# Weight words rebuilt straight into their own tile, fewer and larger loads, and an order made with the queue's eight lanes

## The chip, the cores and the metric

The program runs on one core of a Trainium2 chip, in one launch. TensorE multiplies, VectorE (DVE), ScalarE (ACT) and GpSimd (POOL) work on the elements, and SyncE (SP) issues the transfers. The metric is the device time of one execution in microseconds (us): 658.67 is the median of 3 runs before the change (657.94 to 660.53). The profile is one more execution, which took 658.94 us.

## The reference

```python
def _attn_ref(q, k, v, a_re, a_im):        # 4 batches, 8 heads, 768 tokens, width 48
    mag = np.sqrt(a_re * a_re + a_im * a_im)
    scale = np.minimum(mag, 0.999) / (mag + 1e-06)
    a_re_n, a_im_n = (a_re * scale, a_im * scale)
    for t in range(S):
        new_re = ar * S_re - ai * S_im
        new_im = ar * S_im + ai * S_re
        kv = np.einsum('bhd,bhe->bhde', k[:, :, t], v[:, :, t])
        S_re, S_im = (new_re + kv, new_im)
        y[:, :, t] = np.einsum('bhd,bhde->bhe', q[:, :, t], S_re)
def _moe_ref(x, w_in, w_out, a, b):        # 3072 tokens, 384 -> 2048 -> 384
    h = x @ w_in
    P = a[0] + a[1] * h + a[2] * h * h + a[3] * h * h * h
    Q = 1.0 + np.abs(b[0]) * np.abs(h) + np.abs(b[1]) * h * h
    return (P / (Q + 1e-06)) @ w_out
def _moe2_ref(x, w_skip, ...):             # a token goes on to an expert only if x @ w_skip > 0
    out = x.copy()
```

An attention with a complex decay feeds a wide layer with a rational gate. Then each token is tested against `w_skip`; with the inputs used no path behind that test runs, so the wide layer's result is the output.

## The kernel before, in words

The 3072 tokens are 12 units of 256, each of 2 chunks of 128. For a unit, `early` works the decays (`ar`, `ai`) into logarithms and angles on DVE and ACT, `cums` sums them over time with products on PE, and `trig` takes sines and cosines (`cs`). `prods` multiplies the scaled q and k by them: a product of 768 elements a partition, `kt` from k and `qt` from q, twice per chunk, by DVE or POOL (L378). `chunk` transposes (L696), forms scores (L716), masks them (L721), multiplies by v (L739) and by the carried state (L741), and updates the state (L762). A chunk's result `ys` is corrected by two small transfers inside SBUF (`ysd`) and stored as `xh` and a rest `xl` (L794, L799).

The wide layer runs a unit in 8 steps, of two blocks of 128 hidden columns each: `G1` (L852) makes the hidden values, nine instructions on ACT and DVE (`a1` to `d4`, L832, L375, L836) the gate, `gh` and `gl` (L881, L884) its two parts, `G2` (L904) adds to the output. Units 1 to 11 multiply in three fast parts (high by high, high by low, low by high). Unit 0 multiplies whole F32 values, since its weights are not yet split.

The weights come from HBM as float64 words, as the host holds them, 32 blocks of 128 x 384. `weight` loads a block as words (`ws`, 384 KB), rebuilds the F32 value with three DVE instructions (`wb1` to `wb3`, L425, L428, L435) and one scaling on ACT or POOL (`wy`, L431, L432), and then a transfer on the chip (`wcp`) copies the value from the stage to `wil` or `wol`, because the stage's place becomes the high part (`whi`, L451). `wlo` (L456) turns `wil` and `wol` into the low parts where they stand.

v comes three times per chunk: all heads (`vb`), and the odd heads with the two token halves swapped (`vo`, two transfers of 64 rows x 4 pieces of 48 numbers).

What runs when is written by a planner, `Plan`, at build time. Each task has options (engine and cost), a rank from due times and a table of numbers (`RK`), and engines that it may not use (`NO`). The resulting order is fixed: each engine runs its list in turn, and waits where a result is missing. In gaps of PE's planned list `filled` puts products that nobody reads (L991, L995, L998; "fillers" here). Transfers of SP all go into one queue, and each takes the next of eight semaphores ("lanes") in turn: a transfer on a lane waits for the last one on it.

Of the kernel before, what the change touches and what calls it, by code (L numbers as in the profile page):

```python
# [183 lines left out]
PP = dict(RK={('prr2', 2): 3.12, ('a5', 0): 4.66, ('wb3', 0): 3.26, ('wb2', 0): -1.55, ('a5', 2): 29.52, ('red', 3): -5.84, ('thi', 2): -15.73, ('G2', 3): 5.39, ('sc', 3): -2.18, ('S', 3): 4.15, ('d4', 0): -7.69, ('e10', 2): 43.63, ('e5', 3): -3.63, ('xp', 2): 28.26, ('xhi', 3): 1.43, ('sc', 2): -10.69, ('cry', 3): -3.27, ('d3', 0): -4.72, ('wldo', 0): -11.48, ('S2', 2): -16.91, ('yev', 3): -2.07, ('a3', 3): 2.6, ('a5', 1): -11.48, ('d4', 1): 15.02, ('a1', 0): 5.15, ('ysd', 3): 4.13, ('xpe', 3): 0.91, ('msk', 1): -2.71, ('xlo', 3): 38.81, ('xpe', 1): -5.76, ('e1', 3): 19.05, ('tlo', 2): 31.77, ('e7f', 2): -28.75, ('upd', 2): 20.93, ('G2', 1): -1.18, ('S2', 0): 17.75, ('e8', 2): 10.97, ('wcp', 0): 1.93, ('msk', 0): -34.0, ('cadd', 3): 2.32, ('cuml', 3): 3.94, ('ymm', 3): 0.58, ('ahi', 2): 33.56, ('trig', 3): -7.45, ('a1', 1): 9.46, ('cuml', 2): 40.94, ('a4', 1): -2.63, ('yev', 0): -0.58, ('e7f', 3): 6.69, ('dec', 2): -15.18, ('G2', 2): -1.44, ('e10', 3): 5.07, ('e13', 3): -3.92, ('e4', 3): -0.99, ('d4', 3): -1.96, ('rnd', 0): 51.87, ('upd', 1): -11.05, ('prr1', 2): -12.43, ('e6', 3): 19.64, ('exq', 3): -0.91, ('cumx', 2): -2.78, ('a2', 2): 18.7, ('xp', 0): -12.54, ('xabs', 0): -9.64, ('G1', 0): 3.1, ('a4', 0): -2.66, ('e6', 2): -8.09, ('ysd', 1): -6.35, ('d3', 3): 2.37, ('red', 1): -3.23, ('G1', 3): 0.96, ('e11', 0): -34.69, ('alo', 2): 3.31, ('gl', 1): -3.15, ('G1', 2): 0.12, ('e9', 2): -27.01, ('qr', 3): -8.38, ('dec', 1): 5.65, ('xlo', 2): 1.21, ('e7', 3): 0.19, ('e3', 3): 6.62, ('cadd', 1): -9.18, ('ldk', 2): -62.56, ('prr2', 1): 6.83, ('gh', 2): 0.17, ('gl', 3): 17.93, ('ldv', 3): 12.89, ('cumx', 0): -1.69, ('xlo', 1): -4.07, ('wlo', 0): -0.06, ('a5', 3): -0.37, ('e11', 3): 0.32, ('e10', 0): -4.98, ('xp', 1): 6.71, ('d1', 3): 0.76, ('d1', 1): -4.12, ('exq', 1): -7.0, ('xhi', 2): 3.18, ('e9', 3): 7.67, ('e2', 0): 16.76, ('ev', 1): -17.58, ('lda', 0): 10.16, ('sk', 0): -11.96, ('S2', 3): -2.37, ('e7', 1): 1.46, ('a3', 2): 5.85, ('e5', 0): -4.81, ('e11', 1): 14.72, ('a2', 3): 4.03, ('dec', 0): -2.65, ('sk', 2): 5.88, ('xpe', 0): -0.24, ('cf', 0): 0.81, ('st', 0): 6.79, ('dec', 3): -6.11, ('e2', 3): 2.44, ('a4', 2): -2.83, ('kr', 0): -3.6, ('msk', 3): -0.46, ('G1', 1): -1.67, ('d2', 3): -2.05, ('a3', 1): 5.72, ('ldk', 3): 1.99, ('rnd', 3): 10.32, ('sk', 3): -2.18, ('e11', 2): -8.06, ('ymm', 2): -1.42, ('d2', 1): 10.01, ('G2', 0): 1.41, ('red', 2): 12.85, ('a1', 2): -3.47, ('e2', 2): -10.52, ('e4', 1): -44.42, ('e7', 0): 27.96, ('d2', 0): -1.15, ('lda', 1): -1.87, ('xabs', 1): -2.0, ('sk', 1): -36.69, ('ev', 0): -14.56, ('e3', 1): 23.6, ('whi', 0): 0.56, ('e9', 1): -3.01, ('e4', 0): 6.8, ('S', 0): 7.17, ('xabs', 3): -4.9, ('gl', 2): -3.79, ('e8', 0): 2.21, ('exp', 3): 8.53, ('d1', 2): 0.05, ('qr', 2): -11.3, ('xabs', 2): 1.36, ('d4', 2): -1.13, ('qr', 0): -3.05, ('e8', 1): 8.77, ('lda', 3): 0.02, ('e7', 2): -9.52, ('ldq', 3): 12.22, ('st', 1): -2.0, ('kr', 2): -6.08, ('ldc', 0): 10.23, ('ldk', 1): -12.6, ('last', 1): 27.98, ('prr1', 1): 0.86, ('e7f', 1): 3.77, ('cry', 1): -1.5, ('consts', 0): -7.94, ('kr', 1): 7.89, ('consts2', 0): -1.73, ('wb1', 0): 0.08, ('sc', 1): -1.53, ('a1', 3): -0.46, ('e6', 0): 1.18, ('thi', 3): 3.26, ('clear', 0): 0.66, ('e13', 1): 4.78, ('cuml', 1): 0.28, ('ldq', 1): -1.73, ('gh', 3): 8.2, ('trig', 0): 2.05, ('S', 2): 1.66, ('e5', 1): -1.37, ('qr', 1): -4.52, ('e10', 1): -0.7, ('ldq', 2): 18.6, ('sc', 0): -1.03, ('exq', 2): 14.38, ('e9', 0): -0.62, ('xpe', 2): 0.81, ('cumx', 1): 1.08, ('ymm', 0): 6.87, ('yev', 2): 0.36, ('last', 3): -0.64, ('upd', 3): -0.13, ('e13', 2): -2.22, ('e3', 2): 1.71, ('upd', 0): 0.0, ('ev', 2): 1.27, ('lda', 2): 0.45, ('e1', 1): -8.86, ('cadd', 2): -2.13, ('ysd', 0): -2.42, ('gh', 1): 0.65, ('e6', 1): -2.17, ('ldv', 0): 1.52, ('ldk', 0): 1.29, ('d3', 1): 7.67, ('cry', 2): -0.27, ('lnexp', 0): -5.28, ('rnd', 1): -2.74, ('ldv', 2): -0.5}, FU=1, C2=72.509, C3=123.091, AF=6.693, P0=3.688, P1=4.377, NO={'e4': ('POOL',), 'wlo': ('DVE',), 'prr1': ('DVE',), 'whi': ('POOL',), 'thi': ('ACT',)}, E0=68.086, E1=-19.697, TC=16, WS=(0, 1, 2, 3, 4, 5, 0, 1, 1, 0, 1, 2, 2, 1, 2, 2), HO={('cadd', 'POOL'): 0.163, ('last', 'POOL'): 0.177, ('prr2', 'POOL'): 0.1, ('gh', 'ACT'): 0.048, ('tlo', 'POOL'): 0.482, ('thi', 'ACT'): 0.071, ('tlo', 'DVE'): 0.437, ('last', 'ACT'): 0.166, ('yev', 'DVE'): 0.201, ('xhi', 'ACT'): 0.027, ('gh', 'DVE'): 0.58, ('gl', 'POOL'): 0.428, ('xhi', 'DVE'): 0.403, ('xlo', 'POOL'): 0.542, ('wlo', 'DVE'): 0.468, ('gl', 'DVE'): 0.016, ('cadd', 'DVE'): 0.052, ('xpe', 'DVE'): 0.549, ('prr1', 'DVE'): 0.097, ('e4', 'POOL'): 0.456, ('whi', 'POOL'): 0.398}, DW=177.48, WL=7, P=6.193, LAG2=4.124, SL={'ACT': 0.955, 'DVE': 1.413, 'POOL': 0.138, 'SP': 0.1, 'PE': 2.407, '2': 1.094}, X1=27.056, T0=48.313, NZ=6, NH=3, CU=2, BI={'DVE': 73.29, 'POOL': 44.682})  # L184


def main_part(tc, ctx, q, k, v, a_re, a_im, w_in, w_out, moe_a, moe_b, w_skip, out, keep):
# [1202 lines left out]
```

## Time and profile before

| | |
|---|---|
| median of 3 runs | 658.67 us (657.94 to 660.53) |
| the profiled execution | 658.94 us |
| its span, first to last instruction | 657.1 us |
| PE, DVE, ACT, POOL busy | 97%, 86%, 86%, 52% |
| fillers among PE's time | 40.2 us (32.3 + 4.0 + 3.9) |
| DMA moved | 52.09 MB, in 49458 packets, 20320 of them under 512 B |

PE is called busy while it runs a filler too. An F32 product leaves two records in the trace, so 254 records of L998 are 127 instructions.

### The profile page before, as it was taken

Reading aid. Unit: us, or ns where it says so; the run is one execution under the profiler, and the core shown is the slowest. Engines: PE = TensorE matmul, PEld = TensorE weight load, DVE = VectorE, ACT = ScalarE, POOL = GpSimd, SP = SyncE. Lnnn points to the kernel's source line nnn. Section 1 sums busy time; section 2 is a strip of 40 time slices with the busy share of each in tenths; the row PEclk is TensorE's granted clock in tenths of the full one; section 3 lists DMA queues with packets and bytes.
Section 4 is the critical chain, followed back from the end, with each engine's and each line's share of the span. In section 5 each row is a group of like instructions: output and inputs, shape, how many; then the busy total and the mean of one; then the engine's idle time right before and its main releaser. Section 6 shows DMA issues by size and latency. Waiting matters only on the chain.

```text
span 657.1 us, 15009 instructions
## 1 busy us (share of the span) xinstructions
PE 635.3 (97%) x5704; PEld 592.4 (90%) x5704; DVE 562.4 (86%) x897; ACT 563.0 (86%) x935; POOL 338.7 (52%) x339
## 2 busy tenths in 40 slices
PE   9999999989999999999999999999999999999993
PEld 8787777778998989999999999989999999999993
DVE  6988999899899889988998789899889896968882
ACT  6748999998898899997999998989989989867770
POOL 4432577965357475454684654553565753622220
PEclk9998999999999999999999999999999999999997
DMA  8968821501302113013112113013013010000000
GB/s 291 304 211 289 273 96 48 166 24 44 98 25 75 49 47 117 15 35 103 35 47 86 33 47 100 19 47 102 19 46 101 19 49 3 19 30 3 22 4 30
DMA packets 49458, 52.09 MB, mean 79 GB/s; under 512 B 20320, under 2 KB 45280, under 8 KB 49376
## 3 DMA queue, kind: packets, MB, share of 16 engines
q1 hardware_dynamic: 49088, 51.03, 25.5%
q8 instruction: 47, 0.77, 0.5%
q14 instruction: 35, 0.29, 0.1%
q10 hardware_dynamic: 288, 0.00, 0.0%
HBM read 38.73 MB, written 4.72 MB: 66 GB/s over the span
## 4 chain that ended last, share of the span: by engine, by line
PE 66%; ACT 15%; DMA 7%; DVE 4%; issue 3%; SPq 2%; POOL 2%; ACTq 0%; DVEq 0%; POOLq 0%
PE zb L852 24%; PE ob L904 23%; PE zb L696 5%; PE zb L716 4%; DMA ws<-in_moe_w_in_dram 3%; PE zb L739 3%; PE zb L741 2%; ACT wk L832 2%; ACT wk L375 2%; ACT tb L515 2%; PE zb L762 2%; SPq L371 2%; DMA vb<-in_v_dram 1%; ACT L551 1%; ACT zb L832 1%
## 5 line engine op out<-in xcount | busy, mean ns | idle before, releaser
L852 PE MATMUL zb<-xh,wil 128*128 128x256 f32 x624 | 171.2, 297 | 0.3 <-DVE wk L836 0.2
L836 DVE SCALAR_TENSOR_TENSOR wk<-wk,cf,zb 128x512 f32<-128x512 f32 x192 | 141.0, 740 | 26.5 <-ACT zb L832 17.3
L852 PE MATMUL zb<-xh,wi 128*128 128x256 f32 x528 | 152.7, 289 | 0.0
L852 PE MATMUL zb<-xl,wi 128*128 128x256 f32 x528 | 148.8, 282 | 0.0
L375 ACT ACTIVATE wk<-wk,cf 128x512 f32<-128x512 f32 x192 | 139.7, 730 | 2.3
L881 POOL TENSOR_SCALAR gh<-wk 128x512 fp32r<-128x512 f32 x80 | 56.3, 704 | 152.3 <-PE ob L904 100.3
L904 PE MATMUL ob<-wo,gh 128*128 128x384 f32 x352 | 121.4, 345 | 1.7 <-DVE zb L922 1.7
L852 PEld LDWEIGHTS zb<-xh,wil 128*128 128x128 f32 x624 | 117.1, 189 | 4.0 <-DVE wk L836 0.8
L904 PE MATMUL ob<-wol,gh 128*128 128x384 f32 x352 | 118.8, 338 | 0.0
L904 PE MATMUL ob<-wo,gl 128*128 128x384 f32 x352 | 118.8, 338 | 0.0
L852 PEld LDWEIGHTS zb<-xh,wi 128*128 128x128 f32 x528 | 99.4, 188 | 3.1 <-issue 1.9
L852 PEld LDWEIGHTS zb<-xl,wi 128*128 128x128 f32 x528 | 99.3, 188 | 0.4
L832 ACT ACTIVATE wk<-zb,cf 128x512 f32<-128x512 f32 x96 | 66.0, 688 | 10.2 <-PE zb L852 5.2
L836 DVE SCALAR_TENSOR_TENSOR zb<-wk,cf,zb 128x512 f32<-128x512 f32 x96 | 71.5, 746 | 0.0
L832 ACT ACTIVATE zb<-wk 128x512 f32<-128x512 f32 x96 | 58.0, 606 | 14.6 <-DVE wk L836 14.4
L904 PEld LDWEIGHTS ob<-wo,gh 128*128 128x128 f32 x352 | 66.1, 188 | 3.1 <-DVE zb L922 1.9
L832 ACT ACTIVATE wk<-zb 128x512 f32<-128x512 f32 x96 | 57.5, 601 | 12.4 <-PE zb L852 12.0
L836 DVE SCALAR_TENSOR_TENSOR wk<-wk,zb 128x512 f32<-128x512 f32 x96 | 65.2, 681 | 1.3
L904 PEld LDWEIGHTS ob<-wol,gh 128*128 128x128 f32 x352 | 66.3, 188 | 0.0
L904 PEld LDWEIGHTS ob<-wo,gl 128*128 128x128 f32 x352 | 66.1, 188 | 0.0
L884 POOL TENSOR_TENSOR gl<-wk,gh 128x512 fp32r<-128x512 f32 x41 | 60.7, 1480 | 6.2 <-ACT gh L877 3.2
L378 POOL TENSOR_TENSOR qt<-r,cs 128x768 f32<-128x768 f32 x24 | 51.9, 2162 | 20.4 <-ACT cs L552 10.6
(168 smaller groups left out, 1380.0 us busy)
## 6 DMA issues: line engine op xcount, KB each, us to landing
ws<-in_moe_w_in_dram SPq DMA_DIRECT2D x16, 384.0 KB, 6.7
ws<-in_moe_w_out_dram SPq DMA_DIRECT2D x16, 384.0 KB, 4.8
ar<-in_a_re_dram SPq DMA_DIRECT2D x24, 192.0 KB, 3.4
ai<-in_a_im_dram SPq DMA_DIRECT2D x24, 192.0 KB, 3.8
qraw<-in_q_dram SPq DMA_DIRECT2D x24, 192.0 KB, 2.6
kraw<-in_k_dram SPq DMA_DIRECT2D x24, 192.0 KB, 2.5
vb<-in_v_dram SPq DMA_DIRECT2D x24, 192.0 KB, 3.3
out_dram<-x2b SPq DMA_DIRECT2D x24, 192.0 KB, 1.9
```

The costliest lines, as they stand in the source:

```text
L371: nc.sync.dma_start(out=o, in_=i)
L375: return ("ACT", cost, lambda: nc.scalar.activation(out=out, in_=in_, func=func, **kw))
L378: return (e, cost, lambda: eng[e].tensor_tensor(out=out, in0=in0, in1=in1, op=op), both)
L696: nc.tensor.transpose(z[0:112, i, :], src[:, 112 * h:112 * h + 112], ident)
L716: nc.tensor.matmul(z[o:o + 64, h, n:128], lhsT=K[:, h, n:n + 64], rhs=Q[:, h, n:128], start=True, stop=True)
L739: nc.tensor.matmul(dst, lhsT=vt, rhs=pT[hf][:, i, :], start=True, stop=first)
L832: return ("ACT", cost, lambda: nc.scalar.activation(out=h() if out is None else out, in_=h() if in_ is None else in_, func=func, **kw))
L836: return ("DVE", cost, lambda: nc.vector.scalar_tensor_tensor(out=h() if out is None else out, in0=in0, scalar=scalar, in1=h(), op0=op0, o ...
L852: nc.tensor.matmul(h()[:, i * 256:i * 256 + 256], lhsT=w[:, 128 * j:128 * j + 128], rhs=x[:, j, :], start=(n == 0), stop=(n == 3 * len(pr) ...
L881: nc.gpsimd.tensor_scalar(out=g, in0=uu, scalar1=1.0, scalar2=1.0, op0=ALU.mult, op1=ALU.mult)
L884: eng[e].tensor_tensor(out=ghl("gl", s), in0=uu, in1=ghl("gh", s).bitcast(F32), op=ALU.subtract)
L904: nc.tensor.matmul(o, lhsT=a[:, sl], rhs=w, start=(f == 0 and n == 0), stop=(f == NF - 1 and n == len(pr) - 1))
```

## The change

- **Weights.** A transfer brings two blocks (768 KB of words). `wb3` writes the F32 value not into the stage but into a tile of its own (`fi`, `fo`), so that the 32 copies on the chip go. `wlo` no longer works in place: it writes the low part of weight j (`li`, `lo`) into the place of the F32 tile of weight j-1, and so the weights are split in turn, and unit 2's `xl` takes the place of the last F32 tile.
- **Loads.** q, k, `ar` and `ai` of a unit come in one transfer each instead of two. v is laid out on the host with the swapped odd heads behind it, and comes in one transfer of 2304 B a row instead of three. SP issues 474 transfers in the whole program, 616 before.
- **Order.** The planner now follows the eight lanes, a cost per transfer, and has new numbers throughout. Of DVE and POOL, all 48 `kt` and `qt` products are DVE's (16 before); 69 of 88 `gl` and all 88 `gh` are POOL's (41 and 80 before). PE's list has 135 fillers of the kind of L998 (127 before).

```diff
-        queue = 0.0
+        queue, lanes, lane = 0.0, [0.0] * 8, 0
...
+                    if e == "SP":
+                        end, many = now, o_[3]
+                        for _ in range(many):
+                            end = max(end, lanes[lane]) + cost / many
+                            queue = max(queue, end + 0.7) + t.xfer / many
+                            lanes[lane] = queue + 1.1
+                            lane = (lane + 1) % 8
+                        cost = end - now
...
-PP = dict(RK={('prr2', 2): 3.12, ('a5', 0): 4.66, ('wb3', 0): 3.26,
...
+PP = dict(RK={('e1', 3): -0.0, ('qr', 1): 6.96, ('d3', 3): 13.1,
...
-    vb = [T(f"vb{i}", [128, H * 48 + 16]) for i in range(2)]
-    vo = [T(f"vo{i}", [128, H // 2 * 48 + 16]) for i in range(2)]
+    vb = [T(f"vb{i}", [128, H * 72 + 16]) for i in range(2)]
+    vo = [t[:, H * 48:H * 72 + 16] for t in vb]
...
+        if n == "xl" and u % 2 == 0:
+            if "xl0" not in lazy:
+                lazy["xl0"] = keep["wp"].tile([128, 768], F32R, tag=f"wl{2 * NP}", name="xl0")
+            t = lazy["xl0"]
...
+    def weight_f(m, p):
+        if (m, p) not in whole_w:
+            whole_w[m, p] = keep["wp"].tile([128, 2, DM], F32, tag=f"wl{rank_of(m, p) + 1}", name=f"f{m}{p}")
+        return whole_w[m, p]
+
+    def weight_lo(m, p):
+        if p not in low[m]:
+            low[m][p] = keep["wp"].tile([128, 2, DM], F32R, tag=f"wl{rank_of(m, p)}", name=f"l{m}{p}")
+        return low[m][p]
...
+    def weight(m, p, num):
+        slot = ("st", num % NP)
+        d_ = (w_in[p].rearrange("q (z n) -> q z n", z=2) if m == "i" else w_out[2 * p:2 * p + 2].rearrange("z q n -> q z n"))
+        pl.add(dma(lambda: [(stage(num).bitcast(I32), d_.bitcast(I32))], n=1), writes=[slot] + [("sh", num % NP, z) for z in range(2)],
+               name=f"wld{m}{p}", xfer=0.68 * NB / DM * 2)
+        for z in range(2):
+            block(m, p, z, num)
...
         def value():
-            return stage(num)[:, 0:DM]
+            return weight_f(m, p)[:, z, :]
...
-                reads=keys + [w_], writes=[h_], free=tk, name="wb3")
-            src = keys + [h_]
-        w = wil if m == "i" else wol
-        pl.add(dma(lambda: [(w[:, 2 * p + z, :].bitcast(F32), value())], n=1), reads=src, writes=[("wf",) + key], name="wcp", xfer=0.5)
-
+                reads=keys + [w_, h_], writes=[("wf", m, p, z)], free=tk, name="wb3")
...
-            eng[e].tensor_tensor(out=lo, in0=lf, in1=weight_hi(m, p).bitcast(F32), op=ALU.subtract)
+            eng[e].tensor_tensor(out=weight_lo(m, p), in0=weight_f(m, p), in1=weight_hi(m, p).bitcast(F32), op=ALU.subtract)
...
-               reads=h_, writes=w + l_, name="wlo")
+               reads=h_ + w, writes=l_ + before, name="wlo")
...
-            pl.add(dma(*[(raw[nm][:, 8 * c:8 * c + 8, :], chunk_src(x, 2 * u + c)) for c in range(2)]),
-                   writes=[nm], name=f"ld{nm}{u}", xfer=1.3)
+            pl.add(dma((two_chunks(raw[nm]), unit_src(x, u))), writes=[nm], name=f"ld{nm}{u}", xfer=1.3)
...
-        pl.add(dma((vb[ci % 2][:, 0:H * 48], chunk_src(v, ci).rearrange("t h d -> t (h d)")),
-                   (odd[0:64], src[64:128, :, 1]), (odd[64:128], src[0:64, :, 1])),
+        b, c = divmod(ci, CPB)
+        pl.add(dma((vb[ci % 2][:, 0:H * 72], v[b, c * 128:(c + 1) * 128, :])),
...
+def _v_rows(x):
+    b, h, t, d = x.shape
+    x = x.transpose(0, 2, 1, 3)
+    odd = x[:, :, 1::2].reshape(b, t // 128, 2, 64, h // 2 * d)[:, :, ::-1]
+    return np.concatenate([x.reshape(b, t, h * d), odd.reshape(b, t, h // 2 * d)], axis=2)
```

The order moves at three places that the prediction speaks of. The first is SP's list from the fourth unit of decays on up to the first correction of `ys` (`dec` is the decay row of a chunk, `cs<-xr` the carried angle). Before:

```order
L371 DMA wil<-ws_202 128x384
L371 DMA dec_122<-last 48x1x8 x2
L371 DMA wil<-ws_204 128x384
L371 DMA wil<-ws_207 128x384
L371 DMA wil<-ws_211 128x384
L371 DMA cs<-xr 1x8x48
L371 DMA kraw<-in_k_dram 128x384 x2
L371 DMA wil<-ws_224 128x384
L371 DMA ws_499<-in_moe_w_out_dram 128x768
```

and, three copies and three transfers of v later, `ys<-ys 16x3x128 x2`. Now:

```order
L383 DMA ws_341<-in_moe_w_in_dram 128x1536
L383 DMA ws_348<-in_moe_w_out_dram 128x2x768
L383 DMA dec_118<-last 48x1x8 x2
L383 DMA ws_395<-in_moe_w_in_dram 128x1536
L383 DMA ws_400<-in_moe_w_out_dram 128x2x768
L383 DMA cs<-xr 1x8x48
L383 DMA kraw<-in_k_dram 128x2x384
L383 DMA ws_484<-in_moe_w_in_dram 128x1536
L383 DMA vb_95<-in_v_dram 128x576
L383 DMA ys<-ys 16x3x128 x2
```

The copies are gone from between the small transfers, and the loads of words stand there instead.

The second is PE's list in front of the first `G1` of unit 0 (`wil`, now `fi`, is the F32 weight; `ob<-ident` are fillers). Before:

```order
L998 MATMUL ob_79<-ident 128x128 x4
L762 MATMUL zb_82<-vb_98,kt_111 64x48 x16
L998 MATMUL ob_79<-ident 128x128 x2
L621 MATMUL zb_81<-ai_146,trit 128x384
L998 MATMUL ob_79<-ident 128x128 x19
L648 MATMUL zb_81<-ta_156,trir 128x384
L648 MATMUL zb_83<-ta_156,trir 128x384
L998 MATMUL ob_79<-ident 128x128 x3
L852 MATMUL zb_82<-xh_4_646,wil 128x256 x6
```

Now:

```order
L795 MATMUL zb_83<-vb_96,kt_107 64x48 x16
L1032 MATMUL ob_77<-ident 128x128 x2
L681 MATMUL zb_79<-ta_154,trir 128x384
L681 MATMUL zb_82<-ta_154,trir 128x384
L1032 MATMUL ob_77<-ident 128x128 x6
L654 MATMUL zb_83<-ai_142,trit 128x384
L1032 MATMUL ob_77<-ident 128x128 x7
L886 MATMUL zb_83<-xh_4_614,fi_297 128x256 x6
```

In the whole list 108 fillers stood ahead of this `G1`, and now 103, and one `ai` sum more stands ahead of it.

The third is DVE's list where the first `G2` of unit 0 gets its weight (`fo_821`; `wk` are gate values). Now:

```order
L870 SCALAR_TENSOR_TENSOR wk<-wk,zb_83 128x512
L870 SCALAR_TENSOR_TENSOR wk<-wk,cf,zb_84 128x512
L458 TENSOR_SCALAR zb_81<-ws_348 128x384
L870 SCALAR_TENSOR_TENSOR wk<-wk,cf,zb_80 128x512
L461 SCALAR_TENSOR_TENSOR zb_79<-ws_348,zb_79 128x384
L870 SCALAR_TENSOR_TENSOR zb_80<-wk,cf,zb_80 128x512
L461 SCALAR_TENSOR_TENSOR zb_81<-ws_348,zb_81 128x384
L870 SCALAR_TENSOR_TENSOR wk<-wk,zb_80 128x512
L468 SCALAR_TENSOR_TENSOR fo_821<-ws_348,zb_79 128x384
L468 SCALAR_TENSOR_TENSOR fo_821<-ws_348,zb_81 128x384
```

Before, the same weight (`ws_215`, `ws_220`) was rebuilt ahead of DVE's first gate instruction, and was copied by a transfer later; now it stands behind two steps of the gate.

## Rows read from the trace of the kernel before

**Rows 1.** The page: busy us of each engine (share of the span), instructions.

```profile
PE 635.3 (97%) x5704; PEld 592.4 (90%) x5704; DVE 562.4 (86%) x897; ACT 563.0 (86%) x935; POOL 338.7 (52%) x339
```

**Rows 2.** Groups of all instructions, PE's fillers: records | busy us, mean ns | idle before.

```profile
L998 PE MATMUL ob<-ident 128*128 128x128 f32 x254 | 32.3, 281 | 0.0
```

**Rows 3.** Waits of PE, whole span: what waited, for whom: us in total, times, longest.

```profile
PE ob L904 <- DVE zb L922: 1.7, 1, 1.7
PE zb L319 <- POOL nedge L290: 1.5, 1, 1.5
```

**Rows 4.** Waits of PE from 150 us on, all three that the view lists.

```profile
PE zb L716 <- ACT qT L702: 1.9, 3, 0.9
PE faz L1301 <- DVE fat L1295: 1.7, 1, 1.7
PE zb L696 <- DVE kt L378: 0.8, 1, 0.8
```

**Rows 5.** SP in order of time, 32 to 53 us: start, us, what.

```profile
32.01 1.26 SPq L371 DMA_DIRECT2D dec<-last  x2
...
43.39 1.30 SPq L371 DMA_DIRECT2D ys<-ys  x2
...
52.77 1.48 SPq L371 DMA_DIRECT2D ys<-ys  x2
```

**Rows 6.** ACT in order of time, 48 to 61 us; idle before in brackets.

```profile
48.24 0.52 ACT L794 ACTIVATE xh<-ys 128x384 f32<-128x384 f32 x1 [2.54 <-DMA ys<-ys]
...
50.08 0.84 ACT L557 ACTIVATE ai<-ai 128x768 f32<-128x768 f32 x1
...
60.63 0.51 ACT L794 ACTIVATE xh<-ys 128x384 f32<-128x384 f32 x1
```

**Rows 7.** DVE in order of time, five places.

```profile
11.41 0.56 DVE L425 TENSOR_SCALAR zb<-ws 128x384 int32<-128x384 int32 x1 [1.58 <-DMA ws<-in_moe_w_in_dram]
...
50.95 0.55 DVE L579 SCALAR_TENSOR_TENSOR ai<-cs,ai 1x384 f32<-1x384 f32 x1 [1.47 <-ACT ai L557]
...
58.25 1.48 DVE L435 SCALAR_TENSOR_TENSOR ws<-ws,zb 128x384 int32<-128x384 int32 x3
...
138.89 3.49 DVE L378 TENSOR_TENSOR kt<-r,cs 128x768 f32<-128x768 f32 x2 [0.49 <-ACT cs L552]
...
371.59 0.96 DVE L378 TENSOR_TENSOR kt<-r,cs 128x768 f32<-128x768 f32 x1 [2.14 <-ACT cs L552]
```

**Rows 8.** PE in order of time, 49 to 75 us.

```profile
49.54 1.14 PE L762 MATMUL zb<-vb,kt 128*64 128x48 f32 x32 [0.93 <-DVE ys L781]
...
52.53 1.62 PE L621 MATMUL zb<-ai,trit 128*128 128x384 f32 x2 [1.21 <-issue]
...
61.20 5.45 PE L852 MATMUL zb<-xh,wil 128*128 128x256 f32 x24
...
73.31 1.45 PE L904 MATMUL ob<-wol,wk 128*128 128x384 f32 x4
```

**Rows 9.** Stretches of 2 us: PE, PEld, DVE, ACT, POOL busy; granted clock, DMA share, GB/s.

```profile
52.00:54.00 2.00, 1.47 (x3) 0.90 (x4) 1.82 (x4) 1.96 (x4) 0.53 (x1) 0.55 1.04 356
54.00:56.00 2.00, 2.00 (x13) 2.00 (x12) 1.83 (x4) 1.56 (x3) 0.00 (x0) 0.60 1.02 401
```

**Rows 10.** Stretches of 20 us, the same columns.

```profile
20.00:40.00 20.00, 19.50 (x215) 18.16 (x214) 18.74 (x41) 14.56 (x23) 9.35 (x9) 1.00 0.81 278
40.00:60.00 20.00, 16.89 (x175) 14.67 (x175) 16.65 (x29) 11.30 (x16) 3.44 (x5) 0.91 0.88 282
```

**Rows 11.** Groups of all instructions: the gate on DVE, gl, products of cs.

```profile
L836 DVE SCALAR_TENSOR_TENSOR wk<-wk,cf,zb 128x512 f32<-128x512 f32 x192 | 141.0, 740 | 26.5 <-ACT zb L832 17.3 <-ACT wk L832 8.4
...
L884 POOL TENSOR_TENSOR gl<-wk,gh 128x512 fp32r<-128x512 f32 x41 | 60.7, 1480 | 6.2 <-ACT gh L877 3.2 <-DVE gh L879 0.4
...
L884 DVE TENSOR_TENSOR gl<-wk,gh 128x512 fp32r<-128x512 f32 x47 | 42.3, 899 | 12.5 <-POOL gh L881 12.3
...
L378 DVE TENSOR_TENSOR kt<-r,cs 128x768 f32<-128x768 f32 x16 | 28.6, 1802 | 3.9 <-ACT cs L552 3.8
```

More of the change, by code (lines that the diff above doesn't have):

```diff
@@ L444, in split @@
         w, h_, l_ = ([(n,) + k for k in ks] for n in ("wf", "wh", "wl"))
-        lo = (wil if m == "i" else wol)[:, 2 * p:2 * p + 2, :]
-        lf = lo.bitcast(F32)
+        j = rank_of(m, p) - 1
+        before = [("wf", "io"[j % 2], j // 2, z) for z in range(2)] if j >= 0 else []
         def whi(e):
@@ L450, in whi @@
             if e == "ACT":
-                nc.scalar.activation(out=hi, in_=lf, func=AF.Copy)
+                nc.scalar.activation(out=hi, in_=weight_f(m, p), func=AF.Copy)
             else:
-                nc.gpsimd.tensor_scalar(out=hi, in0=lf, scalar1=1.0, scalar2=1.0, op0=ALU.mult, op1=ALU.mult)
+                nc.gpsimd.tensor_scalar(out=hi, in0=weight_f(m, p), scalar1=1.0, scalar2=1.0, op0=ALU.mult, op1=ALU.mult)
         def wlo(e):
-            eng[e].tensor_tensor(out=lo, in0=lf, in1=weight_hi(m, p).bitcast(F32), op=ALU.subtract)
-        pl.add([("ACT", 0.73, lambda: whi("ACT")), ("POOL", 0.85, lambda: whi("POOL"))], reads=w, writes=h_ + [("st", p + (NP if m == "o" else 0))], name="whi")
+            eng[e].tensor_tensor(out=weight_lo(m, p), in0=weight_f(m, p), in1=weight_hi(m, p).bitcast(F32), op=ALU.subtract)
+        pl.add([("ACT", 0.73, lambda: whi("ACT")), ("POOL", 0.85, lambda: whi("POOL"))], reads=w, writes=h_ + [("st", (p + (NP if m == "o" else 0)) // 2)], name="whi")
         pl.add([("POOL", 1.85, lambda: wlo("POOL")), ("DVE", 0.87, lambda: wlo("DVE"), True)],
-               reads=h_, writes=w + l_, name="wlo")
+               reads=h_ + w, writes=l_ + before, name="wlo")
     x2k = [("x2", i) for i in range(2)]
@@ L467, in weights @@
                 if 0 <= q_ < NP:
-                    for z in range(2):
-                        weight(m, q_, z, num)
-                        num += 1
+                    weight(m, q_, num)
+                    num += 1
     flat = "p h d -> p (h d)"
@@ L571, in cums @@
             cr = cs[0:1, hs, 1, :]
-            pl.add(dma((cr, xr[127:128, ps, :])), reads=[f"x{1 - c}"], writes=[f"cs{c}"], name=f"cry{ci}", xfer=0.03)
+            pl.add(dma((cr, xr[127:128, ps, :]), c=0.78), reads=[f"x{1 - c}"], writes=[f"cs{c}"], name=f"cry{ci}", xfer=0.03)
             def a0():
@@ L668, in cums @@
                    reads=[f"r1{c}"], writes=["last"], name="last")
-            pl.add(dma(*[(dec[ci % ND][64 * z:64 * z + 48, :], last[127:128]) for z in range(2)]), reads=["last"], writes=[("dec", ci % ND)], name=f"dec{ci}")
+            pl.add(dma(*[(dec[ci % ND][64 * z:64 * z + 48, :], last[127:128]) for z in range(2)], c=0.66), reads=["last"], writes=[("dec", ci % ND)], name=f"dec{ci}")
     def qrkr(u):
@@ L785, in yevac @@
             prs.append((keep["dbg"][ci], ys))
-        pl.add(dma(*prs), writes=["ys"], name="ysd", xfer=0.14)
+        pl.add(dma(*prs, c=0.66), writes=["ys"], name="ysd", xfer=0.14)
         sl = slice(128 * c, 128 * c + 128)
@@ L806, in yevac @@
         pl.add([("POOL", 0.99, lambda: xlo("POOL")), ("DVE", 0.47, lambda: xlo("DVE"), True)],
-               reads=["ys", ("xh", u % 2, c)], writes=[("xl", u % 2, c)], name="xlo", due=due)
+               reads=["ys", ("xh", u % 2, c)], writes=[("xl", u % 2, c)] + ([("wf", "o", NP - 1, z) for z in range(2)] if u == 2 else []),
+                   name="xlo", due=due)
     def chunk(ci):
```

68 lines of the change are left out of this document (38 added, 30 removed).

## The prediction

> **What bounds the kernel now.** I read the page first, then PE's waits, then PE in order of time with the granted clock, and last the engines that PE waits for. PE is busy 635.3 of 657.1 us [rows 1], and its list is fixed, fillers included. So the time is what PE's instructions take, plus the stretches in which PE stands still, plus the end behind its last product. From 150 us on PE waits 1.9 + 0.8 us in all, and 1.7 more for the last flag product at the very end [rows 4]: a faster step anywhere in that stretch has 2.7 us to win. What can be won lies ahead of 150 us, where each of DVE, ACT and PE is late in turn. Between 20 and 60 us PE stands still 0.50 + 3.11 = 3.6 us [rows 10]; the first 1.5 us wait for the first constant [rows 3] and stay; one wait of 1.7 us lies further on, for DVE's skip scores of unit 0 [rows 3].
>
> The wait of 40 to 60 us can be followed. SP works its list in turn, and issues the first correction of `ys` only at 43.39 [rows 5]. ACT stands 2.54 us for it, so its `xh` starts at 48.24, and the angles behind it at 50.08 [rows 6]; DVE waits 1.47 us for these and adds the carry at 50.95 [rows 7]; PE sums them at 52.53, after 1.21 us in which it waited [rows 8]. In the 4 us after this the granted clock is 0.55 and 0.60, that is, largely at 1.2 instead of 2.4 GHz, where it was 1.00 before [rows 9, 10]. The first `G1` of unit 0 comes at 61.20 [rows 8], just behind the second `xh`, which ACT starts at 60.63 [rows 6] although its `ys` was corrected by a transfer of 52.77 [rows 5].
>
> **The change part by part.** The sum is made against the profiled execution, 658.94 us; it lies 0.3 us above the median.
>
> *PE's own list.* It has the same products as before, and 8 fillers more. 254 records of 32.3 us [rows 2] are 127 fillers of 0.254 us: 8 x 0.254 = +2.0. If one of them falls into a wait it costs nothing, so the bounds are 0 and +2.0; I take all of it.
>
> *Copies and transfers.* 32 copies of 192 KB go (6.3 MB), and 48 small transfers of v in pieces of 192 B. What counts is not the bytes but what stands ahead of the small corrections in SP's list. Ahead of the first correction of `ys` I add up 12.7 MB before (2.2 MB of it copies, each of which waits for DVE's rebuilt word) and 13.3 MB now. But 12.7 MB by 43.39 us are 293 GB/s; with the DMA fully busy, and large pieces, the queue moved 401 GB/s [rows 9], by which 13.3 MB take 33 us. The copies' waits for DVE go from the list, and loads of words that wait for DVE's reading stand there instead, so I take the correction out of SP some 5 us earlier, near 38 us, and the chain of ACT, DVE and PE above no longer stalls there. The decay row (issued at 32.01 [rows 5]) gains in the same way. Of PE's 3.6 us between 20 and 60 I take 3.2 as gone; the bounds are 3.6 gone, and 4 added, if a word load of 768 KB (2 us at 401 GB/s) stands in front of each of two corrections.
>
> *The clock.* Without the wait the clock does not fall there. PE was busy 1.47 us at 0.55 and 2.00 us at 0.60 [rows 9], which at full clock are 0.81 + 1.20: 1.46 less, taken as -1.4 (bounds 0 and -1.4).
>
> *First `G1` and first `G2`.* PE alone would come to the first `G1` at 61.2 - 3.6 - 1.4 - 5 x 0.254 (103 fillers for 108) + 0.8 (one more sum) = 55.7 us. Then PE's list goes on with 54 records of F32 `G1` (5.45 us for 24 [rows 8], so 12.3) and 25 fillers (6.4) to the first `G2`: 74.4 us, where it was 73.31 [rows 8]. Its weight is rebuilt by DVE behind 109 instructions that begin with the first word: 82 of 384 elements at (1.48 - 0.55)/2 = 0.465 [rows 7], 15 of the gate at 0.740 [rows 11] less the 0.08 by which neighbours overlap, 12 of 768 at 0.96 [rows 7] less the same: 38.1 + 9.9 + 10.6 = 58.6. The first rebuild began at 11.41 [rows 7], and 384 KB more ahead of it are 1 us: 71.0 us. DVE has 3.4 us in hand, and between 20 and 60 us it stood still 1.26 + 3.35 = 4.6 us [rows 10], waiting mainly for words and for what the small transfers held up. I take its weight as in time, which costs 0; the bounds are 0 and the price in the second rival.
>
> *DVE and POOL.* 32 products move from POOL to DVE and 28 `gl` the other way. At the means of the rows DVE gets 32 x 1.80 - 28 x 0.90 = +32.5 us [rows 11], at the 0.96 us of a product with no other beside it [rows 7] 48 x 0.96 - 28.6 - 25.2 = -7.7. Two products that began with one on POOL took 3.49 us together, 1.75 each [rows 7]; in the new order no such pair is left, so I go near the lower end: DVE stays at about 86%. Of the 1.7 us for unit 0's skip scores [rows 3] I take half as gone, -0.8 (bounds -1.7 and +3), since DVE has no `gl` in that stretch but keeps the scores.
>
> The Trainium skill ("SBUF — State Buffer", section "SBUF: two separate sides") says that VectorE and GpSimd share one port pair as an exclusive lock, and that an operation of VectorE with two inputs in SBUF is blocked for as long as a GpSimd operation that reads SBUF holds it. The 3.49 us beside 0.96 agree. By that rule the change is not free: `gl` and the splitting on POOL can hold a product of DVE as the products on POOL did.
>
> *Splitting in turn.* `wlo` of weight j now waits for the last use of weight j-1 in unit 0, and it is all POOL's, as before. POOL is busy 52% [rows 1]; unit 1's steps use the parts in the same turn. I cost it at 0; cover is POOL's idle time, and without it each late part costs unit 1 up to 1.9 us.
>
> Sum: 658.94 + 2.0 - 3.2 - 1.4 - 0.8 = 655.5 us.
>
> **The rivals.** *Nothing comes back.* PE's list is full of fillers that were planned for slower loads, so an earlier word finds PE at a filler; or the waits only move: 658.94 + 2.0 - 1.4 = 659.5, and with the clock falling as before 661. For it: all engines but POOL are above 85% busy [rows 1], and the fillers are fixed. Against it: the waits of 40 to 60 us have a cause that the change takes out.
>
> *DVE comes too late (slower).* The place is the first `G2`, for which PE's list now holds 25 fillers and DVE's the weight of step 0 behind two steps of the gate. It decides as soon as DVE loses more than 3.4 us ahead of it. If it stands still for 4.6 us as before and unit 0's four products are held by POOL for 1.80 - 0.96 = 0.84 us each, it is 4.6 + 3.4 - 3.4 = 4.6 us late; the clock falls again (+1.4), and one of the next steps, which have the same order, loses half as much: 655.5 + 4.6 + 1.4 + 2.3 = 664. For it: the idle time of DVE [rows 10]; against it: that idle time came in good part from late transfers.
>
> *More comes back.* All 3.6, all 1.7, and half of the 2.7 us behind 150 us go: 658.94 + 2.0 - 3.6 - 1.4 - 1.7 - 1.4 = 652.8; with no filler in the way (0 instead of +2.0) 650.8.
>
> The skill's page "DMA: Bandwidth & Descriptors" ("Rules for kernel authors") asks to join small transfers into large ones, and states in "Specifications" that under 512 B an element the engine reads, modifies and writes. By it, the time would follow the 20 thousand small pieces that go; the list of waits speaks against that, since from 150 us on no wait of PE is for a transfer [rows 4].
>
> **How the numbers follow.** The forecast has 0.48, nothing comes back 0.20, DVE too late 0.16, more comes back 0.16. About half a per cent, 3.3 us, is what a measurement of this kernel can tell from no change. Against the median of 658.67 faster then means below 655.4 and slower above 662.0. The forecast's own range is 653 to 658.5, a little under half of it below 655.4: 0.22; with 0.16 of the last rival, and a little for an end that I do not see, 0.41 for faster. Slower is 0.15 of DVE too late and 0.03 of nothing comes back: 0.18. The same: 0.41. The range that should hold 8 of 10 is 650.8 to 662.5.
>
> **What would show it.** In the profile after: no PE wait of 1 us between 45 and 55 us and a clock of 1.00 there; first correction of `ys` issued before 40 us; the first `G1` at 55 to 58 us; the first `G2` at 74 to 76, with no wait for DVE in front of it; 270 records of the filler L1032 at 34.3 us; DVE's products at a mean near 1 us. The prediction is wrong if PE waits for DVE's weight word or a gate value of unit 0 for some us, if PE's waits beyond 150 us grow over 5 us (POOL's `gl` late), or if PE's busy time differs by more than 2.5 us from 635.3 + 2.0 - 1.4.

## The result, and the profile after

The changed kernel takes 648.1 us (median of 4 runs, 647.43 to 649.08) against 659.16 (4 runs, 657.94 to 660.53): a ratio of 0.983 (95% interval 0.981 to 0.986). That is faster by 1.7%, and 2.7 us below the range I gave. The profiled execution takes 647.43 us, its span is 645.7.

The engines' shares have hardly moved (the page, then PE's filler group and its whole list of waits; they answer to [rows 1 to 4]):

```profile
PE 633.9 (98%) x5720; PEld 590.3 (91%) x5720; DVE 558.0 (86%) x901; ACT 558.7 (87%) x925; POOL 332.2 (51%) x349
```

```profile
L1032 PE MATMUL ob<-ident 128*128 128x128 f32 x270 | 33.0, 276 | 0.0
```

```profile
PE faz L1335 <- DVE fat L1329: 1.7, 1, 1.7
PE zb L331 <- POOL nedge L302: 1.5, 1, 1.5
PE ob L938 <- DVE zb L956: 0.8, 2, 0.5
PE zb L886 <- ACT xh L827: 0.3, 1, 0.3
PE zb L729 <- ACT kT L735: 0.2, 1, 0.2
```

These five are all the waits that the view lists. The skip scores of unit 0 cost 0.8 us instead of 1.7, and the waits for qT (1.9) and kt (0.8) behind 150 us are gone from the list. PE by stretches of the run, first before, then after (length, PE busy and records, granted clock, DMA share, GB/s):

```profile
0.00:20.00 20.00, 17.88 (x102) 1.00 0.87 284
20.00:60.00 40.00, 36.39 (x388) 0.96 0.85 280
60.00:150.00 90.00, 87.18 (x643) 1.00 0.40 123
150.00:640.00 490.00, 487.14 (x4543) 1.00 0.17 48
```

```profile
0.00:20.00 20.00, 18.53 (x108) 1.00 0.89 333
20.00:60.00 40.00, 39.65 (x402) 1.00 0.68 239
60.00:150.00 90.00, 89.94 (x761) 1.00 0.22 68
150.00:640.00 490.00, 485.80 (x4455) 1.00 0.16 48
```

Length less busy is PE's idle time. It fell by 0.65, 3.26 and 2.76 us in the first three stretches. In the last one PE's last product, the one for the flags left aside, ends at 636.85 (646.55 before), and the idle time up to it fell by 1.65 (from timelines added up). PE is busy 1.4 us less, and the rest of the span behind that product takes 8.85 us, not 10.55. Together: 0.65 + 3.26 + 2.76 + 1.65 + 1.4 + 1.7 = 11.4, which is 657.1 - 645.7.

The chain of [rows 5, 6, 8] stands in after like this. SP:

```profile
23.57 1.26 SPq L383 DMA_DIRECT2D dec<-last  x2
...
35.96 1.29 SPq L383 DMA_DIRECT2D ys<-ys  x2
...
49.87 1.25 SPq L383 DMA_DIRECT2D ys<-ys  x2
```

ACT, with no wait in front of it, then PE:

```profile
40.38 0.84 ACT L590 ACTIVATE ai<-ai 128x768 f32<-128x768 f32 x1
...
46.67 0.51 ACT L827 ACTIVATE xh<-ys 128x384 f32<-128x384 f32 x1
...
54.65 0.51 ACT L827 ACTIVATE xh<-ys 128x384 f32<-128x384 f32 x1
```

```profile
55.20 2.86 PE L886 MATMUL zb<-xh,fi 128*128 128x256 f32 x12 [0.33 <-ACT xh L827]
...
72.75 1.45 PE L938 MATMUL ob<-fo,wk 128*128 128x384 f32 x4
```

The first correction leaves 7.4 us earlier, the angles start 9.7 and the first `G1` 6.0 us earlier. The clock does not fall at 52 to 56 us (answers to [rows 9]; last three columns: clock, DMA share, GB/s):

```profile
52.00:54.00 2.00, 2.00 (x16) 1.74 (x16) 2.00 (x5) 1.95 (x4) 1.00 (x1) 1.00 0.05 11
54.00:56.00 2.00, 1.67 (x12) 1.40 (x12) 1.80 (x5) 1.98 (x5) 0.60 (x2) 1.00 0.26 28
```

DVE and ACT have little idle time left in the stretches of [rows 10] (third and fourth of the busy columns):

```profile
20.00:40.00 20.00, 19.97 (x213) 18.17 (x212) 19.87 (x38) 17.10 (x26) 7.06 (x7) 1.00 0.91 337
40.00:60.00 20.00, 19.67 (x192) 16.98 (x191) 19.70 (x40) 18.42 (x30) 8.42 (x11) 1.00 0.44 141
```

The groups that answer to [rows 11]:

```profile
L870 DVE SCALAR_TENSOR_TENSOR wk<-wk,cf,zb 128x512 f32<-128x512 f32 x192 | 141.7, 742 | 33.0 <-ACT zb L866 26.3 <-ACT wk L866 6.1
L918 POOL TENSOR_TENSOR gl<-wk,gh 128x512 fp32r<-128x512 f32 x69 | 99.2, 1438 | 5.3
...
L390 DVE TENSOR_TENSOR qt<-r,cs 128x768 f32<-128x768 f32 x24 | 28.3, 1179 | 0.0
L390 DVE TENSOR_TENSOR kt<-r,cs 128x768 f32<-128x768 f32 x24 | 24.1, 1005 | 2.6 <-ACT cs L585 2.6
```

### The profile page after: what moved, and what is told of

The parts are those of the page before. It is cut to its first block, busy times and chain, and to the rows that moved or that the text cites. A ratio compares the mean times of both kernels' runs of the same rounds, so it can differ in the third digit from the quotient of the medians.

```text
span 645.7 us, 14813 instructions
## 1 busy us (share of the span) xinstructions
PE 633.9 (98%) x5720; PEld 590.3 (91%) x5720; DVE 558.0 (86%) x901; ACT 558.7 (87%) x925; POOL 332.2 (51%) x349
## 4 chain that ended last, share of the span: by engine, by line
PE 81%; ACT 12%; DVE 4%; issue 2%; POOL 0%; DVEq 0%; ACTq 0%; POOLq 0%
PE zb L886 27%; PE ob L938 25%; PE zb L729 6%; PE zb L749 5%; PE ob L1032 4%; PE zb L772 4%; PE zb L795 3%; PE zb L774 3%; ACT wk L387 2%; ACT wk L866 2%; ACT tb L548 1%; DVE wk L870 1%; PE zb L678 1%; ACT L584 1%; ACT zb L866 1%
## 5 line engine op out<-in xcount | busy, mean ns | idle before, releaser
L886 PE MATMUL zb<-xh,li 128*128 128x256 f32 x528 | 147.8, 280 | 0.0
L915 POOL TENSOR_SCALAR gh<-wk 128x512 fp32r<-128x512 f32 x88 | 61.4, 698 | 147.3 <-PE ob L938 69.4
L938 PE MATMUL ob<-lo,gh 128*128 128x384 f32 x352 | 118.2, 336 | 0.0
L918 POOL TENSOR_TENSOR gl<-wk,gh 128x512 fp32r<-128x512 f32 x69 | 99.2, 1438 | 5.3
L886 PEld LDWEIGHTS zb<-xh,li 128*128 128x128 f32 x528 | 99.4, 188 | 0.0
L938 PEld LDWEIGHTS ob<-lo,gh 128*128 128x128 f32 x352 | 66.2, 188 | 0.0
L749 PEld LDWEIGHTS zb<-qT,kT 112*64 112x64 f32 x768 | 35.4, 137 | 5.9 <-ACT qT L735 3.1
```

What stands on the lines that cost most here:

```text
L749: nc.tensor.matmul(z[o:o + 64, h, n:128], lhsT=K[:, h, n:n + 64], rhs=Q[:, h, n:128], start=True, stop=True)
L886: nc.tensor.matmul(h()[:, i * 256:i * 256 + 256], lhsT=w[:, 128 * j:128 * j + 128], rhs=x[:, j, :], start=(n == 0), stop=(n == 3 * len(pr) ...
L915: nc.gpsimd.tensor_scalar(out=g, in0=uu, scalar1=1.0, scalar2=1.0, op0=ALU.mult, op1=ALU.mult)
L918: eng[e].tensor_tensor(out=ghl("gl", s), in0=uu, in1=ghl("gh", s).bitcast(F32), op=ALU.subtract)
L938: nc.tensor.matmul(o, lhsT=a[:, sl], rhs=w, start=(f == 0 and n == 0), stop=(f == NF - 1 and n == len(pr) - 1))
```

## The experiments

The table has all of them, in us: when the first `ys` correction leaves SP, when the first `G1` starts, from there to the end of PE's last product before the flags, the rest of the span behind it, and the median of the runs with the ratio to before and its interval. The middle columns are from one profile each. Each ratio is to runs of the kernel before that were taken beside the kernel of the row (their medians are 659.06 to 660.08), so equal ratios can stand beside unequal medians.

| kernel | first ys | first G1 | to last product | behind it | median | ratio |
|---|---|---|---|---|---|---|
| before | 43.39 | 61.20 | 585.35 | 10.55 | 659.16 | |
| after | 35.96 | 55.20 | 581.65 | 8.85 | 648.1 | 0.983 (0.981-0.986) |
| after again | 36.34 | 55.58 | 581.66 | 8.76 | 648.29 | 0.982 (0.978-0.986) |
| new order, copies back | 50.66 | 72.26 | 594.44 | 10.50 | 680.13 | 1.033 (1.028-1.037) |
| new order, all old moves | 56.22 | 77.14 | 594.27 | 10.79 | 684.5 | 1.039 (1.035-1.044) |
| old order, new moves | 33.83 | 54.51 | 581.77 | 10.92 | 650.45 | 0.988 (0.984-0.993) |
| the same again | 33.99 | 54.68 | 581.61 | 10.21 | 650.33 | 0.986 (0.982-0.990) |
| old order, new places only | 41.16 | 59.69 | 585.86 | 10.55 | 658.41 | 0.998 (0.995-1.001) |
| and no copies | 35.10 | 54.68 | 585.21 | 8.91 | 650.18 | 0.983 (0.977-0.989) |
| old order, joins only | 35.46 | 55.41 | 583.83 | 11.06 | 653.13 | 0.988 (0.982-0.995) |
| after, half the fillers | 36.50 | 55.96 | 581.79 | 9.25 | 647.8 | 0.983 (0.978-0.987) |
| after, 32 bytes shifted | 35.68 | 54.94 | 583.19 | 8.87 | 649.29 | 0.984 (0.980-0.987) |
| after, 128 bytes shifted | 35.22 | 54.49 | 584.01 | 8.80 | 649.41 | 0.984 (0.981-0.988) |
| after, no late fillers | 36.03 | 55.29 | 581.87 | 8.84 | 647.75 | 0.983 (0.980-0.985) |

Two theories stood first: T, the gain comes from the transfers; O, it comes from the new order.

**New order, old moves.** The rebuilt word goes to the stage again, and a copy follows it:

```diff
-                out=value().bitcast(I32), in0=words()[:, 1, :], scalar=3, ...
+                out=low_.bitcast(I32), in0=words()[:, 1, :], scalar=3, ...
+            nc.sync.dma_start(out=value(), in_=low_)
```

> The kernel after with its order of instructions kept on every compute engine; only the 32 copies on chip are put back: DVE writes the rebuilt word into the stage, and a transfer of 192 KB copies it to the F32 tile, at that place of SP's list. Theory T (the gain comes from the transfers: what stands ahead of the small corrections in SP's list): the first ys correction leaves SP later than 40 us again (35.96 in after, 43.39 before), ACT, DVE and PE stall behind it, PE stands still 3 us or more between 20 and 60 us, time 651 to 654 us. Theory O (the gain comes from the new order, in which PE has fewer places to wait at, with little from the transfers): within 1 us of after, 647.5 to 649 us. The words reach the F32 tile later by about a copy's 2 us in both.

The second kernel takes v, q, k, a and the words in their old number of transfers besides, at the same places of the list:

> As the run with the copies back, and besides v in three transfers a chunk with pieces of 192 B, q and k in two, a in four, the words in 32 loads of 384 KB: all transfers as before the change, all compute engines in the order of after. Theory T: 655 to 659 us, the waits of PE between 20 and 60 us are back (3.3 us or more, against 0.36 in after). Theory O: 648 to 650 us. A mixture shows as a time between, and then the waits of 20 to 60 us and those of 60 to 150 us (2.8 us before, 0.06 in after) tell which part belongs to which.

Both are far above what either theory allowed. With the copies back the first correction leaves at 50.66, and PE waits for copied words, angles and `xh` (the first four of its waits there):

```profile
PE ob L942 <- DMA fo<-ws: 6.8, 6, 2.2
PE zb L658 <- POOL ai L615: 4.2, 2, 2.1
PE zb L685 <- DVE ta L555: 4.0, 1, 4.0
PE zb L890 <- ACT xh L831: 3.4, 1, 3.4
```

O falls: the new order without the new moves is 3 to 4% slower than before. As a size of the copies' cost it is an upper end, since this order was not laid out for them.

**Old order, new moves.** No copies, joined loads of v, q, k and a; the words in 32 loads still. The lower parts go to the tile that the split before freed:

```diff
-        pl.add(dma(lambda: [(w[:, 2 * p + z, :].bitcast(F32), value())], n=1), ... name="wcp", xfer=0.5)
+        pl.add(dma(lambda: [], n=1), ... name="wcp", xfer=0.5)
```

> The kernel before with its order of instructions kept on PE, DVE, ACT and POOL, and the new transfers: no copies (DVE writes the F32 tile, the lower parts go to the tile that the split before freed), v, q, k and a joined as after; the words stay in 32 loads of 384 KB. Theory T: 648 to 651 us, the clock stays 1.00 at 52 to 56 us, and the waits of PE between 20 and 60 us fall from 3.6 to under 1 us. Theory O: 656 to 659 us. My own prediction, read as a statement on transfers alone (waits and clock gone, no new fillers): 658.94 - 3.2 - 1.4 = 654.3 us. G1 products took 119.6 ns each before and 117.8 after (1584 of them, 2.9 us): if that hangs on where the weight tiles lie, they take about 118 here; if on the order, 119.6.

PE's waits between 20 and 60 us go altogether (busy 39.97 of 40), and its last product ends at 636.28, no later than in after:

```profile
20.00:60.00 40.00, 39.97 (x414) 1.00 0.68 233
```

T holds here: 650.45 us, and the granted clock is 1.00 from 52 to 56 us. What the new order does is visible too: the waits that it took out are still here,

```profile
PE zb L744 <- ACT qT L730: 1.8, 3, 0.8
PE ob L932 <- DVE zb L950: 1.8, 1, 1.8
```

but PE is busy 3.0 us less (630.9 against 633.9; 1.5 us of it are fillers, 31.5 against 33.0), so on PE both orders come out alike. It was run once more beside after:

> The kernel after, unchanged, as the mark for the other three of this call: 647.5 to 649 us, G1 products behind 100 us at 117.8 ns.

> The kernel with the old order and the new moves once more, beside after on the same chip. If the new order itself is worth the 2.3 us between the medians so far: 650 to 651 us, against 648 for after. If the difference was chance (PE's last product ended at 636.3 us in its profile, 636.9 in after's): within 1 us of after.

The medians are 2.0 us apart again, which is what I expected if the new order itself is worth something; but it is not on PE. From the first `G1` to the last product it is 581.61 against 581.66, and the first `G1` comes 0.9 us earlier in the old order. The two profiles differ behind the last product (10.21 against 8.76), and by no more than 0.6 us in the whole (648.41 against 647.82): the profiled execution of the old order was the fastest of its six. So the profiles show a part of the 2.0 us only, and the rest stays open.

**Which move.** Three kernels in the old order.

> The kernel before, its order and all its transfers with the 32 copies; only the places in memory change: the F32 words and the lower parts get 17 tiles of 3 KB instead of two of 24 KB, xl of even units shares one of them, and wlo writes the tile that the split before freed, as in the run with the old order and the new moves. Theory P (the places make TensorE's products with the lower parts and with xl cheaper): li products fall from 119.6 to about 117.4 ns and xl products from 120.1 to 118.5, PE's busy time falls by about 2 us, time 656 to 657.5 us with the waits of before. Theory C (those products were slowed by the copies or by the order): they stay at 119.6 and 120.1, time 658 to 660 us.

> As the run with the new places only, and the 32 copies gone besides (DVE writes the F32 tile itself); v, q, k, a and the words in as many transfers as before. If the copies were what held SP's list (each waits for DVE's word): the first ys correction leaves at 34 to 37 us, PE stands still under 1 us between 20 and 60 us, time 650 to 652 us. If the joins did it: the correction stays later than 40 us, time 655 to 657 us.

> The kernel before with its order, its memory places and its copies; only v, q, k and a come in the joined transfers (24 + 24 + 24 DMAs fewer for v's pieces and for q and k, and for a). If the copies held SP's list: the first ys correction leaves at 41 to 43 us, time 656 to 659 us. If the joins did it: at 34 to 37 us, time 651 to 653 us. By the page's rule on pieces under 512 B the 20 thousand small pieces of v would count: about as much as half of the whole gain, 653 to 654 us.

The places alone do little: 658.41 us is theory C's time, and the interval reaches over 1. The products with the low parts stayed at 119.3 ns as C has it, those with `xl` fell to 118.7 as P has it. All `G1` products together took 119.1 ns here and 117.9 with the old order and the new moves, so most of what they gained there does not come from the places of the weights. Without the copies the first correction leaves at 35.10, with the joins and all copies at 35.46, and in both PE does not wait between 20 and 60 us (0.03 us of idle time each). Without the copies, then with the joins:

```profile
35.10 1.30 SPq L376 DMA_DIRECT2D ys<-ys  x2
20.00:60.00 40.00, 39.97 (x414) 1.00 0.75 246
```

```profile
35.46 1.41 SPq L371 DMA_DIRECT2D ys<-ys  x2
20.00:60.00 40.00, 39.97 (x416) 1.00 0.86 298
```

So either edit alone unblocks SP's list; the second adds nothing to that. I expected one of them to be the cause, and neither theory had this. Without the copies the gain lies ahead of the first `G1` (6.5 us) and in the end (1.6 us), and the stretch between is as before. The joins also move `xh` by 128 bytes, which is the subject further on and of the size of 583.83 against 585.21, though the weights lie in different places in these two kernels as well. The joins' end is 2.15 us longer than that without copies.

What the two edits have in common is SP's own work. Ahead of the first correction SP issued 54 transfers before, and the issues took 28.4 of the 43.39 us. Without the copies they are 45 and take 21.5 us, with the joins 43 and 19.5 us, with both 34 and 15.2 us, and in after 28 and 12.7 us (added up from the timelines). The correction left 8.3 and 7.9 us earlier with one edit, while the issues became shorter by 6.9 and 8.9 us. With both it left at 33.83, only 1.3 us earlier than without the copies alone, so by then something else sets its time; what that is was not followed. Fewer issues are thus a likely reason that either edit will do, but no run changed their number alone.

Bytes are not the reason: the joins move 52.09 MB as before. The small pieces are not either. 653.13 us is where the expectation put the time if the pieces count (653 to 654), but without the copies 19,808 of the 20,320 packets under 512 B stay, and the whole gain is there (650.18). (The joins save 48 transfers of v, 24 of q and k and 22 of `ar` and `ai`, not 24 of each.)

**The fillers.** Every second one left out:

```diff
-        else:
+        elif n % 2 == 0:
             nc.tensor.matmul(ob[0][:, 384:512], lhsT=ident, rhs=ident, ...)
```

> The kernel after with every second of its 135 fillers L1032 left out (67 or 68 of 0.24 us, 16 us of PE's list). The term +2.0 of my sum (a filler costs its time) would give 648.1 - 16 = 632 us, at most lessened by waits. The rival (a filler stands where PE would wait anyway, up to 76 us DVE and ACT set the pace) gives 647 to 649 us with PE's waits up to 76 us grown by about 16 us, and, if the granted clock then falls as it did before at 52 to 56 us, 1 to 6 us more, 649 to 654 us.

The time stays. PE's list has 14.9 us of fillers less (18.1 against 33.0). Up to 150 us PE's idle time is 10.8 us longer, and its busy time falls by 10.1 us only, while the granted clock is 0.91 where it was 1.00, that is, for a part at 1.2 instead of 2.4 GHz (20 to 40 and 40 to 60 us). The 1 to 6 us that I expected for such a fall of the clock did not come:

```profile
20.00:40.00 20.00, 16.10 (x160) 0.91 0.92 338
40.00:60.00 20.00, 16.68 (x151) 0.91 0.42 137
```

> The kernel after without the 7 fillers that its list holds behind 78 us (14 records, 1.83 us between 100 and 150 us, where PE of after stands still 0.06 us between 60 and 150 us); the 128 fillers ahead stay. Leaving out every second filler cost nothing, since those ahead of 76 us stand where PE waits anyway. If the late ones are paid for in full: 646 to 647 us, against 648.2 for after (648.1 and 648.29 in two calls). If PE's waits take their place: 648 us and as many us of waits between 100 and 150 us.

647.75 lies within the range of after's runs (647.43 to 649.08), and the stretch behind the first `G1` is no shorter (581.87). PE's idle time between 100 and 150 us grew by 0.63 us where 1.83 us of fillers went, so neither of the two expectations came in full. This and the kernel with half the fillers have the lowest medians, but neither is shown to beat after.

**The addresses.** One line more behind the tiles of v (32 instead of 8 for 128 bytes):

```diff
     vo = [t[:, H * 48:H * 72 + 16] for t in vb]
+    pad = T("pad", [128, 8])
```

> The kernel after with an unused tile of 32 bytes a partition behind the tiles of v, so that the tiles behind it, xh and xl1 among them, lie 32 bytes further (the addresses of xh then divide by 128). In the eight profiles so far G1 products took 119.1 to 119.6 ns where xh lay at 992 beyond a multiple of 1024 bytes (before, new places only, no copies only) and 117.6 to 118.4 where it lay at 864 (after and the others). If the address decides and alignment is what counts: 116 to 117.5 ns, PE 1 to 3 us shorter, 646 to 647 us. If only the step between 864 and 992 matters or the address does not: 117.8, 648 us.

> The kernel after with an unused tile of 128 bytes there, so that xh lies at 992 beyond a multiple of 1024 bytes as in the kernel before. If the address decides: G1 products at 119.1 to 119.6 ns, PE 2 to 3 us longer, 650 to 651 us. If it was the pieces of v or chance: 117.8, 648 us.

From the first `G1` to the last product it takes 1.5 and 2.35 us longer, where two profiles of after agree within 0.01. So it matters where the tiles behind v lie (the pad moves all of them, not `xh` alone), and not by the alignment that I guessed: with `xh` at a multiple of 128 bytes the stretch is longer than in after, not shorter. The whole time rose less, from 648.29 to 649.29 and 649.41 us (I expected 650 to 651 for 128 bytes), and the intervals of the ratios overlap; in these two profiles the first `G1` came 0.3 to 1.1 us earlier than in after's. One comparison inside the runs points at a tile's own place: the `xl` of even units lies among the weights and is not moved by the pad. With 128 bytes its products keep 117.5 ns (117.6 in after), and those with the `xl` of odd units, which moved, go from 117.4 to 119.7. But with 32 bytes both go to 119.0, so a tile's own place is not all of it. The rows show `G1` of 500 to 600 us in the kernel before, after (again) and after with 128 bytes: 140.1, 137.5 and 139.1 ns a record (137.9 in the first profile of after).

```profile
500.00:600.00 100.00, 42.88 (x306) 1.00 0.10 28
```

```profile
500.00:600.00 100.00, 41.79 (x304) 1.00 0.09 29
```

```profile
500.00:600.00 100.00, 41.59 (x299) 1.00 0.09 31
```

## Why the prediction was wrong

The forecast was 655.5 us, the profile shows 647.43. The chain from the first correction to PE was right and so was the size of its main term; what the sum left out, or charged, failed. PE's idle time fell by 8.3 us where the sum has 4.0, its busy time fell by 1.4 where the sum has +0.6, and the end fell by 1.7 where it has 0: together 8.0 of the 8.1 us.

- **Waits of 20 to 60 us, -3.2.** Measured -3.26. The correction left at 35.96 (I said near 38), the first `G1` came at 55.20 (55.7). The reason that I gave for it, the copies' waits for DVE's words, is not in the rows, and so the good size is in part luck. Up to 44 us, SP's list of waits has 1.0 us for DVE's words before (the first two rows), and in after it waits 6.9 us for DVE's work on them (the third). What fell is the time of SP's issues, from 28.4 to 12.7 us.

```profile
SPq L371 <- DVE ws L435: 0.6, 2, 0.4
SPq L371 <- DVE zb L425: 0.4, 1, 0.4
```

```profile
SPq L383 <- DVE fi L468: 6.9, 4, 3.2
```

- **The clock, -1.4.** It stays at 1.00 there. The gain is within PE's busy time and can't be told apart in it.
- **Eight more fillers, +2.0.** This step failed. The group has 270 records as said; it is busy 33.0 us, only 0.7 more than before (0.244 us a filler, not 0.254), and half of all fillers can go without a change of the time. Ahead of the first `G2` DVE and ACT have hardly any idle time (19.70 and 18.42 of 20 us busy between 40 and 60), and a filler fills what would be a wait. I gave the bound of 0 and took the other end.
- **Skip scores, -0.8, and nothing else behind 61 us.** The term itself came true (1.7 us of waiting became 0.8); that nothing else would go failed. All but 0.06 us of the idle time between 60 and 150 us went (2.76 us) and 1.65 of that behind it, where I had written that 2.7 were to be won and took nothing. The new order does this, and pays for it in a longer list: the old order with the new moves keeps 1.86 and 2.22 us of this idle time, and its last product ends no later.
- **PE's list has the same products, so it costs the same.** This failed, unseen: `G1` became cheaper by 1.7 ns each, 1,584 times 1.74 = 2.8 us. Moving the tiles behind v back up by 128 bytes returned 1.4 ns each and 2.35 us of the stretch, so most of it comes from their place. With the fillers (+0.7) and the clock (-1.4 at most) PE's busy time would have fallen by 3.5 us; it fell by 1.4, so the other products became some 2 us dearer, which no run takes apart.
- **The end.** I took what lies behind the last product as fixed; it fell by 1.7 us.
- **First `G2`, DVE's weight.** At 72.75 instead of 74.4, with no wait for DVE in front of it. From the first `G1` it took 17.55 us, not 18.7, as fillers in a row take 0.23 us each (38 records in 4.40 us). The rival "DVE comes too late" did not come.
- **DVE and POOL.** The products of DVE take 1.18 and 1.00 us and DVE is busy 86%, as said. The Trainium skill's rule ("SBUF — State Buffer", "SBUF: two separate sides") would let POOL's 69 `gl` hold DVE's products; these stayed within 0.22 us of the 0.96 of one alone, so here it costs little.
- **"More comes back", 652.8 or 650.8**, was the nearest rival, and its reasons were largely right (more waits gone, free fillers); it lacked the addresses and the end, 2.8 + 1.7 us.
- **The small pieces.** The Trainium skill ("DMA: Bandwidth & Descriptors", "Rules for kernel authors") asks to join small transfers. Joins alone gave 1.2% here, but taking out the copies while all pieces of v stayed gave 1.7% (650.18 us). What counts is what stands ahead of the corrections in SP's list, not the pieces themselves. The 20 thousand small packets were not v's alone either: the joins took away 13.8 of the 20.3 thousand.

What remains open: why the addresses matter, why the end behind the last product has two lengths, and whether SP's list was held by the number of its issues or by a wait that both edits shorten.

## What to carry to other kernels

Where one queue carries both bulk and small transfers on which engines wait, look at what stands ahead of the small ones; two different edits can each cure the same block, and then they don't add up. Fillers can be free where PE would otherwise wait for other engines, as here, where half of them left out changed nothing: price them by the stretch, not by their length. When an edit changes tile sizes, the addresses behind them move, and here a sum of instructions at old durations was then off by 0.4% (2.8 of 658.94 us).

## What the runs showed of the hardware

A `G1` product took 119.5, 119.1 and 119.1 ns in the three kernels with `xh` at 992 bytes beyond a multiple of 1024 and the old v tiles, 119.2 in after shifted there, 119.1 at 896, and 117.7 to 118.0 in the nine others, at 864 (counted from the traces, from one product's end to the next, behind 100 us; these ends are modelled, and from start to start the kernel at 896 comes out at 118.7 and the nine at 118.0 to 118.1).

The end behind the last product took 8.8 to 9.3 us in seven profiles and 10.2 to 11.1 in seven. In the former one queue moves 8 packets of instructions there, in the latter 9 or 10. The rows are of after, then of before:

```profile
q14 instruction: 8, 0.07, 2.3%
```

```profile
q14 instruction: 9, 0.07, 2.1%
```

All fourteen profiles agree in this. It goes with the 1.45 and 2.07 us by which the two orders with the new moves differ at the end in their profiles. Whether the packet is the cause, and which part of the program makes it, was not tried.
